# Window attention, forward and backward: another order of work in the opening and in the tail, and later loads

## The chip, the cores and the metric

The kernel runs on one core of one Trainium2 chip. The metric is the device time of one execution in microseconds (us); of several executions the median is given. A profile is taken of a single execution; its "span" reaches from the first to the last instruction of the program, and the execution's own time is a little longer than the span.

The engines: TensorE (PE in the profile; PEld are its weight loads), VectorE (DVE), ScalarE (ACT), GpSimd (POOL) and SyncE (SP). POOL, SP and ACT also issue DMAs, each in its own program order; an instruction that waits holds up everything behind it on its engine.

## The reference

An 8x8 window attention over an image of 256x256 pixels with C = 384 channels, in bf16, with its gradients. x is cut into 1024 windows of 64 tokens.

```python
qkv = xw @ wqkv                       # xw: (1024, 64, 384)
q, k, v = split(qkv)
p = softmax(q @ k.T * C**-0.5)        # per window, 64 x 64
o = (p @ v) @ wo
```

The kernel returns o and, for a given gradient of o, the gradients of x (out_1), of wqkv (out_2, 384x1152) and of wo (out_3, 384x384).

## The kernel before, in words

The weights are folded first: A2 = Wq Wk^T (scaled), A1 its counterpart with q and k exchanged, so the transpose of A2, A3 = wo Wv^T in the form that the gradient needs, and Bm = Wv wo, so the transpose of A3. With these, a window's scores are x A2 x^T, and no q, k or v is ever formed. To fold them, wqkv (w_sb) and wo (wo_sb) are loaded by one DMA each (L68 on SP, L70 on ACT), transposed on TensorE in groups of three 128x128 blocks (L80 to L89; 9 groups for wqkv, 3 for wo, the results in wqkvT_sb and woT_sb), and multiplied (fold, L91 to L104: 9 products for each of the four).

The tokens are worked through in 128 "quads" (NQ) of QT = 4 tiles of 128 tokens (two windows each). A quad needs x_tok and do_tok (4 DMAs of 96 KB each, load_x L123, load_do L128); xdT, both transposed by DMA (front_transpose L135, issued by SP, two DMA transposes); ygT = the products with A2 (first half, from x) and A3 (second half, from do) (front_project L161, 18 products of 512 columns), and yg, its transpose by DMA (L176, three on SP); the scores (front_scores L179); the softmax and its gradient on VectorE with the exponential on ScalarE (front_softmax, front_exp, front_ds); and zb, the products with A1 and Bm (front_zb L225). The back part of a quad forms W and U (back_uw L273), out and dx (back_out L281, which stores them by 6 DMAs on POOL for each of the two) from these. dx needs yg.

The weight gradients are sums over all tokens: G (from U) and F (from W), each in three blocks of 128 rows. weight_grad (L294) is a chain of TensorE products that accumulate in PSUM, four for each quad covered; at the end of a chain the sum is added to G_acc or F_acc in fp32 by VectorE. One of the six blocks (NCH = 6, chains 0 to 2 for G, 3 to 5 for F) is served in each pass, b % 6, over all quads since it was last served: in passes 6 and later 24 products, before that 4 b.

The order of the work is written out by hand (manual_schedule, L331 to L377): each engine executes its instructions in program order. Pass b of the loop (L345) does the back part of quad b and, in between, the front part of quad b + 1, and it asks for the data of quad b + 4: do on POOL at the top of the pass (L349), behind the stores of the pass before; x on SP (L356), behind the DMA transposes of front_transpose(b + 2) and of yg(b + 1). Quads 0 to 3 are loaded ahead of the loop, by POOL (L332 to L340). Pools: 11 buffers for x, 5 for do, 2 for xdT, yg, zb and ygT, 3 each for the staged stores; of PSUM, 3 places (psT, tag "t") that nearly every product and transpose of TensorE goes through.

After the loop the six chains are finished, in the order of how much they have covered (L375); with pass 127 done, 8, 4, 24, 20, 16 and 12 products are left for chains 0 to 5. VectorE casts G_acc and F_acc to bf16 (Gb, Fb, L380, L382), TensorE transposes both (L389), and twelve groups of three products (last, L393) with ScalarE evictions give the gradients of wqkv and wo, which SP stores with four DMAs (L403, L406).

Of the kernel before, what the change touches and what calls it, by code (L numbers as in the profile page):

```python
# [25 lines left out]
def kernel(  # L26
# [32 lines left out]
    psS = ctx.enter_context(tc.tile_pool(name="psS", bufs=1, space=bass.MemoryType.PSUM))  # L59
    psW = ctx.enter_context(tc.tile_pool(name="psW", bufs=1, space=bass.MemoryType.PSUM))  # L60

    mm = nc.tensor.matmul
    tr = nc.tensor.transpose

    ident = const.tile([P, P], BF16)
    make_identity(nc, ident[:])
    w_sb = const.tile([P, CK, J], BF16)
    nc.sync.dma_start(out=w_sb[:], in_=wqkv.rearrange("(m p) j -> p m j", p=P))  # L68
    wo_sb = const.tile([P, CK, C], BF16)
    nc.scalar.dma_start(out=wo_sb[:], in_=wo.rearrange("(m p) n -> p m n", p=P))  # L70
    woT_sb = const.tile([P, CK, C], BF16)
    A1_sb = const.tile([P, CK, C], BF16)
    A2_sb = const.tile([P, CK, C], BF16)
# [2 lines left out]
    big_sb = const.tile([P, JK * C], BF16)  # L76
    wqkvT_sb = big_sb[:].rearrange("p (j c) -> p j c", j=JK)
    dwqkv_sb = big_sb[:].rearrange("p (m j) -> p m j", m=CK)

    for jm in range(JK):  # L80
        ps_t = psT.tile([P, C], BF16, tag="t")
        for m in range(CK):
            tr(ps_t[:, m * P:(m + 1) * P], w_sb[:, m, jm * P:(jm + 1) * P], ident[:])  # L83
        nc.vector.tensor_copy(out=wqkvT_sb[:, jm, :], in_=ps_t[:])
    for mco in range(CK):
        ps_t = psT.tile([P, C], BF16, tag="t")
        for mc in range(CK):
            tr(ps_t[:, mc * P:(mc + 1) * P], wo_sb[:, mc, mco * P:(mco + 1) * P], ident[:])
        nc.vector.tensor_copy(out=woT_sb[:, mco, :], in_=ps_t[:])  # L89

    def fold(dst, lhs, rhs, mul):  # L91
        for i in range(CK):
            ps_c = psT.tile([P, C], F32, tag="t")
            for mc in range(CK):
                mm(ps_c[:], lhsT=lhs(mc, i), rhs=rhs(mc), start=(mc == 0), stop=(mc == CK - 1))  # L95
            nc.scalar.activation(out=dst[:, i, :], in_=ps_c[:], func=ACT.Copy, scale=mul)

    def cut(i):
        return slice(i * P, (i + 1) * P)

    fold(A2_sb, lambda mc, i: wqkvT_sb[:, mc, cut(i)], lambda mc: wqkvT_sb[:, CK + mc, :], scale)
    fold(A3_sb, lambda mc, i: wo_sb[:, mc, cut(i)], lambda mc: wqkvT_sb[:, 2 * CK + mc, :], 1.0)
    fold(A1_sb, lambda mc, i: wqkvT_sb[:, CK + mc, cut(i)], lambda mc: wqkvT_sb[:, mc, :], scale)
    fold(Bm_sb, lambda mc, i: wqkvT_sb[:, 2 * CK + mc, cut(i)], lambda mc: wo_sb[:, mc, :], 1.0)  # L104

    G_acc = const.tile([P, CK, C], F32)
    F_acc = const.tile([P, CK, C], F32)
# [10 lines left out]
        return ap[0, r0:r0 + WIN, c0:c0 + WIN, :]  # L118

    st = [dict() for _ in range(NQ)]  # L120
    vec, act = nc.vector.tensor_copy, nc.scalar.copy

    def load_x(q, eng):  # L123
        st[q]["x"] = x_tok = tokp.tile([P, QT, C], BF16, name="x_tok")
        for t in range(QT):
            eng.dma_start(out=x_tok[:, t, :], in_=dram(x, q, t))
# [8 lines left out]
    def front_transpose(q):  # L135
        s = st[q]
        s["xdT"] = xdT = quad.tile([P, 2, QT, CK, P], BF16, name="xdT")
        for a, src, n in ((0, s["x"], QT), (1, s["do"], QT - PE_T)):
            if n:
                nc.sync.dma_start_transpose(xdT[:, a, 0:n].rearrange("p t m k -> p (t m) k"),  # L140
                                            src[:, 0:n].rearrange("p t c -> p (t c)"))
# [149 lines left out]

    covered = [0] * NCH

    def weight_grad(c, upto, pool, tag):  # L294
        which, acc = (("U", G_acc), ("W", F_acc))[c // CK]
        ma = c % CK
        first = covered[c] == 0
        todo = [(q, t) for q in range(covered[c], upto) for t in range(QT)]
        covered[c] = upto
        if not todo:  # L300
            return
        ps = pool.tile([P, C], F32, tag=tag, name="ps_dw")
        for k, (q, t) in enumerate(todo):
            s = st[q]
            xt = s["xs"][:, t // 2, :] if t % 2 else s["x"][:, t, :]
            mm(ps[:], lhsT=xt[:, cut(ma)], rhs=s[which][:, t, :],  # L306
               start=(k == 0), stop=(k == len(todo) - 1))
            if k == len(todo) - 1:
                if first:
                    nc.vector.tensor_copy(out=acc[:, ma, :], in_=ps[:])  # L310
                else:
                    nc.vector.tensor_tensor(out=acc[:, ma, :], in0=ps[:], in1=acc[:, ma, :], op=ALU.add)
            yield

    def fill(chain, n):
# [13 lines left out]
        front_zb(q, 3)  # L329

    with tc.manual_schedule(engines={ENG.PE, ENG.Activation, ENG.DVE, ENG.Pool, ENG.SP}):  # L331
        load_x(0, nc.gpsimd)  # L332
        load_do(0)
        load_x(1, nc.gpsimd)
        load_do(1)
        front_transpose(0)
        front_transpose(1)
        for q in (2, 3):
            load_x(q, nc.gpsimd)
            load_do(q)  # L340
        front_project(0)
        front_scores(0)
        front_softmax(0)
        zb_phase(0, 1)
        for b in range(NQ):  # L345
            f = b + 1
            ahead = f < NQ
            if b + 4 < NQ:
                load_do(b + 4)  # L349
            if b + 2 < NQ:  # L350
                front_transpose(b + 2)
            back_transpose(b)
            if ahead:
                front_project(f)
            if b + 4 < NQ:
                load_x(b + 4, nc.sync)  # L356
            chain = weight_grad(b % NCH, b, psW, "w")
            half = 2 * QT * min(b, SPAN) // 4
            back_uw(b, "W", 0, act)
            back_uw(b, "W", 1, vec)  # L360
            swap_halves(b)
            fill(chain, half)
            back_uw(b, "U", 0, act)
            back_uw(b, "U", 1, vec)
            back_out(b, "out", 0, act, out_0)
            for _ in chain:
                pass
            back_out(b, "out", 1, act, out_0)
            back_out(b, "dx", 0, vec, out_1)
            back_out(b, "dx", 1, act, out_1)  # L370
            if ahead:
                front_scores(f)
                front_softmax(f)
                zb_phase(f, f + 1 if f + 1 < NQ else None)
        for c in sorted(range(NCH), key=lambda c: covered[c]):  # L375
            for _ in weight_grad(c, NQ, psT, "t"):
                pass  # L377

    Gb = quad.tile([P, CK, C], BF16, tag="yg", name="Gb")
    nc.vector.tensor_copy(out=Gb[:], in_=G_acc[:])  # L380
    Fb = quad.tile([P, CK, C], BF16, tag="yg", name="Fb")
    nc.vector.tensor_copy(out=Fb[:], in_=F_acc[:])  # L382
    GTb = quad.tile([P, CK, C], BF16, tag="zb", name="GTb")
    FTb = quad.tile([P, CK, C], BF16, tag="zb", name="FTb")
    for src, dst in ((Gb, GTb), (Fb, FTb)):
        for mb in range(CK):
            ps_t = psT.tile([P, C], BF16, tag="t")
            for ma in range(CK):
                tr(ps_t[:, cut(ma)], src[:, ma, cut(mb)], ident[:])  # L389
            nc.vector.tensor_copy(out=dst[:, mb, :], in_=ps_t[:])  # L390
    dwo_sb = quad.tile([P, CK, C], BF16, tag="xdT", name="dwo_sb")

    def last(dst, lhs, rhs, mul):  # L393
        ps_e = psT.tile([P, C], F32, tag="t")
        for mb in range(CK):
            mm(ps_e[:], lhsT=lhs(mb), rhs=rhs(mb), start=(mb == 0), stop=(mb == CK - 1))  # L396
        nc.scalar.activation(out=dst, in_=ps_e[:], func=ACT.Copy, scale=mul)

    for ma in range(CK):
        last(dwqkv_sb[:, ma, 0:C], lambda mb: GTb[:, mb, cut(ma)], lambda mb: w_sb[:, mb, C:2 * C], scale)  # L400
        last(dwqkv_sb[:, ma, C:2 * C], lambda mb: Gb[:, mb, cut(ma)], lambda mb: w_sb[:, mb, 0:C], scale)
        last(dwqkv_sb[:, ma, 2 * C:3 * C], lambda mb: FTb[:, mb, cut(ma)], lambda mb: woT_sb[:, mb, :], 1.0)
        nc.sync.dma_start(out=out_2[cut(ma), :], in_=dwqkv_sb[:, ma, :])  # L403
    for mc in range(CK):
        last(dwo_sb[:, mc, :], lambda mb: w_sb[:, mb, 2 * C + mc * P:2 * C + (mc + 1) * P], lambda mb: Fb[:, mb, :], 1.0)
    nc.sync.dma_start(out=out_3.rearrange("(m p) n -> p m n", p=P), in_=dwo_sb[:])  # L406


# [1 line left out]
_INS = ['x', 'wqkv', 'wo', 'grad_out']  # L410
# [26 lines left out]
```

## Time and profile before

| | us |
|---|---|
| time, median of 3 runs (lowest, highest) | 1992.58 (1989.24, 1993.04) |
| the profiled execution's own time | 1991.48 |
| its span | 1989.7 |
| TensorE busy | 1968.0 (99%) |
| VectorE, ScalarE, GpSimd busy | 1454.9, 1213.7, 1129.6 |
| TensorE's first product starts | 6.56 |
| scores of quad 0, 1, 2, 3, 4, 5, 6 start | 20.7, 35.1, 48.4, 61.9, 79.8, 95.2, 109.8 |
| from there on, from scores to scores | 15.20 |
| the last weight gradient product starts | 1976.27 |

How to read it: "busy" of TensorE is modelled from pipelined products, so 99% does not mean that it works at its peak; what can be read from it is where it is not busy. In a line of a timeline there stand the start, the time taken, the engine, the line of the code, the operation, what is written from what, and in brackets how long the engine had been idle and what ended that. Lines with SPq, ACTq and POOL DMA are issues: their time is that of the issuing, and the data land some us later (medians by the page: x by SP 4.2, do 5.1, yg 5.4, xdT 6.3 and 7.1). The granted clock is the share of TensorE's full clock.

### The profile page before, as it was taken

How to read it: one execution, taken by the hardware profiler on the slowest of the kernel's cores; microseconds unless marked ns; L12 is line 12 of the kernel's file. 1: busy time of each engine (PE TensorE's matmuls, PEld its weight loads, DVE VectorE, ACT ScalarE, POOL GpSimd, SP SyncE). 2: the span in 40 equal slices, each digit the busy share in tenths (PEclk: the TensorE clock that was granted, in tenths of full speed). 3: DMA queues.
4: the chain of work that ended last, by engine and by line, in shares of the span. 5: the costliest groups of instructions: out<-in, count | busy, mean ns of one | idle time of the engine just before them, and what ended most of it. 6: DMA issues, size and time to landing. Idle time of an engine off the chain costs nothing.

```text
span 1989.7 us, 52709 instructions
## 1 busy us (share of the span) xinstructions
PE 1968.0 (99%) x20862; PEld 1061.7 (53%) x20862; DVE 1454.9 (73%) x2713; ACT 1213.7 (61%) x1689; POOL 1129.6 (57%) x2070
## 2 busy tenths in 40 slices
PE   7999999999999999999999999999999999999998
PEld 4455555555555555555555555555555555555554
DVE  5777777777777777777777777777777777777774
ACT  5666566566666666665666666666656666666663
POOL 6555555555555655655665555555556555555552
PEclk9999999999999999999999999999999999999999
DMA  9999999999999999999999999999999999999982
GB/s 217 208 216 214 207 213 211 212 213 200 205 208 208 215 213 206 207 214 204 213 206 208 208 208 219 207 197 222 206 206 211 210 202 204 222 206 211 215 175 73
DMA packets 979287, 408.89 MB, mean 206 GB/s; under 512 B 864352, under 2 KB 953440, under 8 KB 979040
## 3 DMA queue, kind: packets, MB, share of 16 engines
q1 hardware_dynamic: 879568, 252.26, 77.8%
q0 software_dynamic: 99072, 152.96, 31.6%
q8 instruction: 164, 2.69, 0.6%
q14 instruction: 83, 0.68, 0.1%
q10 hardware_dynamic: 400, 0.29, 0.0%
HBM read 101.84 MB, written 101.84 MB: 102 GB/s over the span
## 4 chain that ended last, share of the span: by engine, by line
PE 98%; DMA 1%; DVE 1%; ACT 0%; issue 0%
PE ps_dw L306 26%; PE ps_zb L232 26%; PE ps_yg L171 25%; PE ps_dx L257 6%; PE ps_S L187 6%; PE ps_out L257 3%; PE ps_W L257 3%; PE ps_U L257 3%; DMA yg<-ygT 1%; PE ps_c L95 0%; DMA w_sb<-in_wqkv_dram 0%; PE ps_e L396 0%; DVE W_sb L279 0%; PE ps_t L83 0%; DVE ygT L173 0%
## 5 line engine op out<-in xcount | busy, mean ns | idle before, releaser
L286 POOL DMA_DIRECT2D out_dram<-out_sb x256 | 139.2, 544 | 695.4 <-ACT out_sb L285 689.2
L234 ACT CAST zb<-ps_zb 128x768 bf16<-128x768 f32 x512 | 407.6, 796 | 191.7 <-PE ps_zb L232 172.8
L171 PE MATMUL ps_yg<-xdT,A_sb 128*128 128x512 bf16 x2304 | 518.2, 379 | 0.0
L232 PEld LDWEIGHTS <-xdT 128*128 128x128 bf16 x3072 | 290.3, 98 | 188.1 <-issue 1.0
L171 PEld LDWEIGHTS <-A_sb 128*128 128x128 bf16 x2304 | 225.4, 98 | 258.2
L173 ACT CAST ygT<-ps_yg 128x512 bf16<-128x512 f32 (+1 forms) x384 | 280.2, 730 | 92.1 <-PE ps_yg L171 91.0
L232 PE MATMUL ps_zb<-A_sb,xdT 128*128 128x384 bf16 x1536 | 335.1, 327 | 0.0
L232 PE MATMUL ps_zb<-Bm_sb,xdT 128*128 128x384 bf16 x1536 | 333.8, 326 | 0.0
L285 ACT CAST out_sb<-ps_out 128x768 bf16<-128x768 f32 x256 | 205.0, 801 | 151.6 <-issue 143.3
L131 POOL DMA_DIRECT2D do_tok<-in_grad_out_dram x512 | 274.0, 553 | 28.5 <-issue 14.1
L306 PE MATMUL ps_dw<-U_sb,x_tok 128*128 128x384 bf16 x768 | 251.0, 328 | 0.0
L306 PE MATMUL ps_dw<-W_sb,x_tok 128*128 128x384 bf16 x768 | 251.0, 328 | 0.0
L306 PE MATMUL ps_dw<-U_sb,x_sw 128*128 128x384 bf16 x768 | 249.7, 326 | 0.0
L306 PE MATMUL ps_dw<-W_sb,x_sw 128*128 128x384 bf16 x768 | 249.7, 326 | 0.0
L306 PEld LDWEIGHTS <-x_tok 128*128 128x128 bf16 x1536 | 149.6, 97 | 160.1 <-issue 77.1
L279 ACT CAST U_sb<-ps_U 128x768 bf16<-128x768 f32 x128 | 102.1, 798 | 213.8 <-PE ps_U L257 213.8
L247 DVE STREAM_TRANSPOSE pdsT<-pds 32x256 bf16<-32x256 bf16 x512 | 223.2, 436 | 12.0
L306 PEld LDWEIGHTS <-x_sw 128*128 128x128 bf16 x1536 | 150.3, 98 | 82.8
L209 DVE TENSOR_REDUCE rs<-e 128x4 f32<-128x256 f32 x128 | 53.8, 420 | 172.2 <-ACT e L203 172.2
L173 DVE CAST ygT<-ps_yg 128x1024 bf16<-128x1024 f32 x128 | 156.8, 1225 | 29.9 <-PE ps_yg L171 29.3
L288 POOL DMA_DIRECT2D out_dram<-dx_sb x256 | 144.0, 562 | 37.6 <-DMA out_dram<-out_sb 29.7
L287 POOL DMA_DIRECT2D out_dram<-dx_sb x256 | 144.0, 562 | 25.8 <-DMA out_dram<-out_sb 17.5
(71 smaller groups left out, 2596.5 us busy)
## 6 DMA issues: line engine op xcount, KB each, us to landing
do_tok<-in_grad_out_dram POOLq DMA_DIRECT2D x512, 96.0 KB, 5.1
x_tok<-in_x_dram SPq DMA_DIRECT2D x496, 96.0 KB, 4.2
out_dram<-out_sb POOLq DMA_DIRECT2D x256, 96.0 KB, 4.3
out_dram<-out_sb POOLq DMA_DIRECT2D x512, 48.0 KB, 4.3
out_dram<-dx_sb POOLq DMA_DIRECT2D x256, 96.0 KB, 3.7
out_dram<-dx_sb POOLq DMA_DIRECT2D x512, 48.0 KB, 3.8
yg<-ygT SPq DMA_TRANSPOSE x384, 5.4
xdT<-x_tok SPq DMA_TRANSPOSE x128, 6.3
```

Source lines behind the costliest of these rows:

```text
L131: nc.gpsimd.dma_start(out=do_tok[:, t, :], in_=dram(grad_out, q, t))
L171: mm(ps[:, i], lhsT=A_sb[:, m, cut(j)], rhs=s["xdT"][:, a, :, m, :], start=(m == 0), stop=(m == CK - 1))
L173: copy(out=ygT[:, js[0]:js[0] + len(js), :], in_=ps[:, 0:len(js)])
L232: mm(ps[:, i, 0:C], lhsT=s["xdT"][:, 0, t, m, :], rhs=w[:, m, :], start=(m == 0), stop=(m == CK - 1))
L234: nc.scalar.copy(out=s["zb"][:, t], in_=ps[:, :, 0:C])
L247: nc.vector.transpose(out=dst[h + 32 * c:h + 32 * c + 32, :, r, :], in_=src[h + 32 * r:h + 32 * r + 32, :, c, :])
L257: mm(ps[o, b, 0:C], lhsT=lt[i, t, :], rhs=rt(i, t), start=(k == 0), stop=(k == n - 1))
L285: copy(out=o[:], in_=ps[:, :, 0:C])
L286: nc.gpsimd.dma_start(out=dram(dst, q, 2 * p), in_=o[:, 0, :])
L287: nc.gpsimd.dma_start(out=dram_half(dst, q, 2 * p + 1, 1), in_=o[LO, 1, :])
L288: nc.gpsimd.dma_start(out=dram_half(dst, q, 2 * p + 1, 0), in_=o[HI, 1, :])
L306: mm(ps[:], lhsT=xt[:, cut(ma)], rhs=s[which][:, t, :], start=(k == 0), stop=(k == len(todo) - 1))
```

## The change

In the opening:
- w is loaded by three DMAs (its q, k and v columns), still by SP; x(0) is loaded by ACT, and wo after it; the identity is made after these are issued; do(0), x(1), do(1) stay on POOL.
- VectorE fills a tile with zeros, and TensorE does ten products of 384 columns with it into an unused PSUM place.
- wqkv's blocks are transposed third by third (turn_w), copied out by VectorE and ScalarE in turn. A2 is folded after the first two thirds, A3 after the last. A1 and Bm are not folded any more: they are transposed from A2 and A3 on TensorE (turn, three groups each), after the scores of quad 0 and ahead of its zb; so are the three groups of woT. ScalarE copies all nine out.
- POOL copies one column of A3 into the zero tile ahead of the loads of quad 2, so that these wait for A3. Quad 3 isn't loaded ahead of the loop.

In the loop: passes 0 to 5 ask for one quad, b + 3, with x and do both on POOL at the top; pass 6 asks for two, 9 and 10, and from pass 7 on it is b + 4 as before, x on SP.

In the tail: the chains are finished in the order 0 to 5; the last addition of each writes bf16 straight to Gb or Fb, and the two casts go. G is transposed after chain 3, the products of G follow, two after chain 4 and four after chain 5; then F's transposes, the three products for wo's gradient and the three with FTb. Evictions alternate between ScalarE and VectorE, and the stores are five DMAs of SP (three of them of the q and k columns of a row block, one of out_3, one of a v block), and one each of POOL and ACT.

```diff
-    make_identity(nc, ident[:])
-    nc.sync.dma_start(out=w_sb[:], in_=wqkv.rearrange("(m p) j -> p m j", p=P))
-    nc.scalar.dma_start(out=wo_sb[:], in_=wo.rearrange("(m p) n -> p m n", p=P))
-    for jm in range(JK):
...
-        nc.vector.tensor_copy(out=woT_sb[:, mco, :], in_=ps_t[:])
+    def turn(dst, src, copies):
+        for i in range(CK):
+            ps_t = psT.tile([P, C], BF16, tag="t", name="ps_t")
+            for m in range(CK):
+                tr(ps_t[:, cut(m)], src(m, i), ident[:])
+            copies[i % len(copies)](out=dst(i), in_=ps_t[:])
...
-    fold(A2_sb, lambda mc, i: wqkvT_sb[:, mc, cut(i)], lambda mc: wqkvT_sb[:, CK + mc, :], scale)
-    fold(A3_sb, lambda mc, i: wo_sb[:, mc, cut(i)], lambda mc: wqkvT_sb[:, 2 * CK + mc, :], 1.0)
-    fold(A1_sb, lambda mc, i: wqkvT_sb[:, CK + mc, cut(i)], lambda mc: wqkvT_sb[:, mc, :], scale)
-    fold(Bm_sb, lambda mc, i: wqkvT_sb[:, 2 * CK + mc, cut(i)], lambda mc: wo_sb[:, mc, :], 1.0)
+    def turn_w(k):
+        turn(lambda i: wqkvT_sb[:, k * CK + i, :],
+             lambda m, i: w_sb[:, m, k * C + i * P:k * C + (i + 1) * P], (vec, act))
...
-        load_x(0, nc.gpsimd)
+        for k in range(3):
+            nc.sync.dma_start(out=w_sb[:, :, part(k)], in_=wqkv.rearrange("(m p) j -> p m j", p=P)[:, :, part(k)])
+        load_x(0, nc.scalar)
+        nc.scalar.dma_start(out=wo_sb[:], in_=wo.rearrange("(m p) n -> p m n", p=P))
+        make_identity(nc, ident[:])
         load_do(0)
         load_x(1, nc.gpsimd)
         load_do(1)
+        nc.vector.memset(idle_sb[:], 0.0)
+        ps_i = psT.tile([P, C], F32, tag="t", name="ps_i")
+        for _ in range(10):
+            mm(ps_i[:], lhsT=idle_sb[:, 0:P], rhs=idle_sb[:], start=True, stop=True)
         front_transpose(0)
         front_transpose(1)
-        for q in (2, 3):
-            load_x(q, nc.gpsimd)
-            load_do(q)
+        turn_w(0)
+        turn_w(1)
+        fold(A2_sb, lambda mc, i: wqkvT_sb[:, mc, cut(i)], lambda mc: wqkvT_sb[:, CK + mc, :], scale)
+        turn_w(2)
+        fold(A3_sb, lambda mc, i: wo_sb[:, mc, cut(i)], lambda mc: wqkvT_sb[:, 2 * CK + mc, :], 1.0)
+        nc.gpsimd.tensor_copy(out=idle_sb[:, 0:1], in_=A3_sb[:, CK - 1, 0:1])
+        load_x(2, nc.gpsimd)
+        load_do(2)
         front_project(0)
         front_scores(0)
         front_softmax(0)
+        turn(lambda i: A1_sb[:, i, :], lambda m, i: A2_sb[:, m, cut(i)], (act,))
+        turn(lambda i: Bm_sb[:, i, :], lambda m, i: A3_sb[:, m, cut(i)], (act,))
+        turn(lambda i: woT_sb[:, i, :], lambda m, i: wo_sb[:, m, cut(i)], (act,))
         zb_phase(0, 1)
+        loaded = 3
         for b in range(NQ):
...
-            if b + 4 < NQ:
-                load_do(b + 4)
+            early = b < SPAN
+            todo = range(loaded, min(b + (4 if early else 5), NQ))
+            loaded += len(todo)
+            for q in todo:
+                if early:
+                    load_x(q, nc.gpsimd)
+                load_do(q)
...
-            if b + 4 < NQ:
-                load_x(b + 4, nc.sync)
+            for q in todo:
+                if not early:
+                    load_x(q, nc.sync)
...
-        for c in sorted(range(NCH), key=lambda c: covered[c]):
-            for _ in weight_grad(c, NQ, psT, "t"):
+        def flush(c):
+            for _ in weight_grad(c, NQ, psT, "t", Gb if c < CK else Fb):
                 pass
...
-    nc.vector.tensor_copy(out=Gb[:], in_=G_acc[:])
-    nc.vector.tensor_copy(out=Fb[:], in_=F_acc[:])
...
+        for c in range(CK + 1):
+            flush(c)
+        turn(lambda i: GTb[:, i, :], lambda m, i: Gb[:, m, cut(i)], (act,))
+        flush(CK + 1)
+        last_qk(0)
+        flush(CK + 2)
+        last_qk(1)
+        last_qk(2)
+        turn(lambda i: FTb[:, i, :], lambda m, i: Fb[:, m, cut(i)], (act, vec))
+        for mc in range(CK):
+            last(dwo_sb[:, mc, :], lambda mb: w_sb[:, mb, 2 * C + mc * P:2 * C + (mc + 1) * P], lambda mb: Fb[:, mb, :],
+                 1.0, (act, vec, act)[mc])
+        nc.sync.dma_start(out=out_3.rearrange("(m p) n -> p m n", p=P), in_=dwo_sb[:])
+        for ma in range(CK):
+            last(dwqkv_sb[:, ma, part(2)], lambda mb: FTb[:, mb, cut(ma)], lambda mb: woT_sb[:, mb, :],
+                 1.0, (vec, act, vec)[ma])
+            (nc.gpsimd, nc.sync, nc.scalar)[ma].dma_start(out=out_2[cut(ma), part(2)], in_=dwqkv_sb[:, ma, part(2)])
```

weight_grad gets an argument out, to which the last addition is written in place of acc; last takes the engine of its eviction; last_qk(ma) does the q and the k product of row block ma, evicts one by ScalarE and one by VectorE, and stores both by one DMA of SP.

More of the change, by code (lines that the diff above doesn't have):

```diff
@@ L60 @@
     psW = ctx.enter_context(tc.tile_pool(name="psW", bufs=1, space=bass.MemoryType.PSUM))
+    vec, act = nc.vector.tensor_copy, nc.scalar.copy
     mm = nc.tensor.matmul
@@ L78, with cut, part @@
     dwqkv_sb = big_sb[:].rearrange("p (m j) -> p m j", m=CK)
-    for jm in range(JK):
[L81 to L88, printed above, removed]
-        nc.vector.tensor_copy(out=woT_sb[:, mco, :], in_=ps_t[:])
+    idle_sb = const.tile([P, C], BF16)
+    def cut(i):
+        return slice(i * P, (i + 1) * P)
+    def part(i):
+        return slice(i * C, (i + 1) * C)
+    def turn(dst, src, copies):
[4 more added lines that the diff above has]
+            copies[i % len(copies)](out=dst(i), in_=ps_t[:])
     def fold(dst, lhs, rhs, mul):
         for i in range(CK):
-            ps_c = psT.tile([P, C], F32, tag="t")
+            ps_c = psT.tile([P, C], F32, tag="t", name="ps_c")
             for mc in range(CK):
@@ L96, in fold @@
             nc.scalar.activation(out=dst[:, i, :], in_=ps_c[:], func=ACT.Copy, scale=mul)
-    def cut(i):
-        return slice(i * P, (i + 1) * P)
-    fold(A2_sb, lambda mc, i: wqkvT_sb[:, mc, cut(i)], lambda mc: wqkvT_sb[:, CK + mc, :], scale)
-    fold(A3_sb, lambda mc, i: wo_sb[:, mc, cut(i)], lambda mc: wqkvT_sb[:, 2 * CK + mc, :], 1.0)
-    fold(A1_sb, lambda mc, i: wqkvT_sb[:, CK + mc, cut(i)], lambda mc: wqkvT_sb[:, mc, :], scale)
-    fold(Bm_sb, lambda mc, i: wqkvT_sb[:, 2 * CK + mc, cut(i)], lambda mc: wo_sb[:, mc, :], 1.0)
+    def turn_w(k):
+        turn(lambda i: wqkvT_sb[:, k * CK + i, :],
+             lambda m, i: w_sb[:, m, k * C + i * P:k * C + (i + 1) * P], (vec, act))
     G_acc = const.tile([P, CK, C], F32)
@@ L120 @@
     st = [dict() for _ in range(NQ)]
-    vec, act = nc.vector.tensor_copy, nc.scalar.copy
     def load_x(q, eng):
@@ L292, with weight_grad @@
     covered = [0] * NCH
-    def weight_grad(c, upto, pool, tag):
+    def weight_grad(c, upto, pool, tag, out=None):
         which, acc = (("U", G_acc), ("W", F_acc))[c // CK]
@@ L308, in weight_grad @@
             if k == len(todo) - 1:
+                to = acc if out is None else out
                 if first:
-                    nc.vector.tensor_copy(out=acc[:, ma, :], in_=ps[:])
+                    nc.vector.tensor_copy(out=to[:, ma, :], in_=ps[:])
                 else:
-                    nc.vector.tensor_tensor(out=acc[:, ma, :], in0=ps[:], in1=acc[:, ma, :], op=ALU.add)
+                    nc.vector.tensor_tensor(out=to[:, ma, :], in0=ps[:], in1=acc[:, ma, :], op=ALU.add)
             yield
@@ L374 @@
                 zb_phase(f, f + 1 if f + 1 < NQ else None)
-        for c in sorted(range(NCH), key=lambda c: covered[c]):
-            for _ in weight_grad(c, NQ, psT, "t"):
-                pass
-    Gb = quad.tile([P, CK, C], BF16, tag="yg", name="Gb")
-    nc.vector.tensor_copy(out=Gb[:], in_=G_acc[:])
-    Fb = quad.tile([P, CK, C], BF16, tag="yg", name="Fb")
-    nc.vector.tensor_copy(out=Fb[:], in_=F_acc[:])
-    GTb = quad.tile([P, CK, C], BF16, tag="zb", name="GTb")
-    FTb = quad.tile([P, CK, C], BF16, tag="zb", name="FTb")
@@ L385 @@
[L385 to L405, printed above, removed]
@@ L406 @@
-    nc.sync.dma_start(out=out_3.rearrange("(m p) n -> p m n", p=P), in_=dwo_sb[:])
+        Gb = quad.tile([P, CK, C], BF16, tag="yg", name="Gb")
+        Fb = quad.tile([P, CK, C], BF16, tag="yg", name="Fb")
+        GTb = quad.tile([P, CK, C], BF16, tag="zb", name="GTb")
+        FTb = quad.tile([P, CK, C], BF16, tag="zb", name="FTb")
+        dwo_sb = quad.tile([P, CK, C], BF16, tag="xdT", name="dwo_sb")
+        def flush(c):
+            for _ in weight_grad(c, NQ, psT, "t", Gb if c < CK else Fb):
+                pass
@@ new lines, in last, with last_qk @@
+        def last(dst, lhs, rhs, mul, copy):
+            ps_e = psT.tile([P, C], F32, tag="t", name="ps_e")
+            for mb in range(CK):
+                mm(ps_e[:], lhsT=lhs(mb), rhs=rhs(mb), start=(mb == 0), stop=(mb == CK - 1))
+            if copy is act:
+                nc.scalar.activation(out=dst, in_=ps_e[:], func=ACT.Copy, scale=mul)
+            else:
+                nc.vector.tensor_scalar_mul(out=dst, in0=ps_e[:], scalar1=mul)
+        def last_qk(ma):
+            last(dwqkv_sb[:, ma, part(0)], lambda mb: GTb[:, mb, cut(ma)], lambda mb: w_sb[:, mb, part(1)], scale, act)
+            last(dwqkv_sb[:, ma, part(1)], lambda mb: Gb[:, mb, cut(ma)], lambda mb: w_sb[:, mb, part(0)], scale, vec)
+            nc.sync.dma_start(out=out_2[cut(ma), 0:2 * C], in_=dwqkv_sb[:, ma, 0:2 * C])
```

## The prediction

> **What bounds the kernel now.** I read the page's chain first, then the timelines of the opening and the end, then the waits, then SP's own timeline.
>
> ```profile
> PE 98%; DMA 1%; DVE 1%; ACT 0%; issue 0%
> PE ps_dw L306 26%; PE ps_zb L232 26%; PE ps_yg L171 25%; PE ps_dx L257 6%; PE ps_S L187 6%; PE ps_out L257 3%; PE ps_W L257 3%; PE ps_U L257 3%; DMA yg<-ygT 1%; PE ps_c L95 0%; DMA w_sb<-in_wqkv_dram 0%; PE ps_e L396 0%; DVE W_sb L279 0%; PE ps_t L83 0%; DVE ygT L173 0%
> ```
>
> TensorE is the chain. From the sixth pass on, the scores (L187) start every 15.20 us, without exception, to the end. The change leaves these passes alone, so it can only win in the first 110 us and the last 27. There the chain names two things that are not TensorE: `yg<-ygT`, 1% though one stall made it, and the first weights.
>
> The opening, TensorE's timeline (start, us, what):
>
> ```profile
> 6.56 3.06 PE L83 MATMUL ps_t<-ident,w_sb 128*128 128x128 bf16 x27 [6.56 <-DMA w_sb<-in_wqkv_dram]
> 9.43 1.15 PE L88 MATMUL ps_t<-ident,wo_sb 128*128 128x128 bf16 x9
> 10.39 2.13 PE L95 MATMUL ps_c<-big_sb 128*128 128x384 bf16 x9
> ...
> 16.75 4.05 PE L171 MATMUL ps_yg<-xdT,A_sb 128*128 128x512 bf16 x18
> ```
>
> It waits 6.56 us for the weights, then works without a hole to the first projection; scores start at 20.72, the first zb at 22.58, the second projection at 26.49.
>
> The early stall, TensorE's and then SP's timeline:
>
> ```profile
> 78.83 0.36 PE L257 MATMUL ps_dx<-yg,pds 64*64 64x384 bf16 x4 [3.47 <-DMA yg<-ygT]
> ```
>
> ```profile
> 58.15 2.36 SPq L140 DMA_TRANSPOSE xdT<-x_tok  x1
> 60.70 3.02 SPq L140 DMA_TRANSPOSE xdT<-do_tok  x1
> 63.81 6.64 SPq L176 DMA_TRANSPOSE yg<-ygT  x3
> 70.50 3.10 SPq L126 DMA_DIRECT2D x_tok<-in_x_dram  x4
> ```
>
> The dx products of pass 3 wait 3.47 us for yg(3), which SP began to issue only at 63.81, though its ygT had been evicted by 58.6: SP was still at an x load and two transposes. SP issues back to back from 20 to 200 us. After the stall the granted clock is half from 79.69 to 83.10 (3.41 us): 1.7 us more. The stall costs 5.2.
>
> The end, a timeline:
>
> ```profile
> 1976.27 0.33 PE L306 MATMUL ps_dw<-U_sb,x_sw 128*128 128x384 bf16 x1
> ...
> 1978.04 0.68 PE L389 MATMUL ps_t<-ident,Gb 128*128 128x128 bf16 x9 [1.45 <-DVE Gb L380]
> ...
> 1984.89 1.47 ACT L397 ACTIVATE dwo_sb<-ps_e 128x384 bf16<-128x384 f32 x3
> 1986.38 0.38 SPq L406 DMA_DIRECT2D out_dram<-dwo_sb  x1
> ```
>
> TensorE waits for two casts on VectorE, then twelve products are paced by ScalarE's 0.49 us evictions.
>
> **Opening.** Before scores(0), 18 fold products (A1, Bm; 18 x 0.163 = 2.9 us) and nine transposes of wo go. w in thirds brings the first columns sooner; x(0), now issued by ScalarE ahead of wo, is no longer behind all of w, so its transpose on SP starts near 6 instead of 7.97. The weight path (nine groups of transposes, copied alternately by VectorE, 0.32 us, and ScalarE, taken as 0.49 from the 128x384 evictions, then two folds of 1.5) is done by about 12 and lies beside the next wait: the projection's second half needs the transposed do(0). By 8.94 before had landed w, wo, x(0) and do(0); the same bytes go first after, so do(0) lands near 8.9. Its transpose took 3.2 us to issue (9.77 to 12.96), and the one of x(0) landed 3.8 us after its issue ended (9.60; the trace marks its completion at 13.44, and so for every landing below). I take 14 for the landing, a little under 8.9 + 3.2 + 3.8 because fewer loads compete; ends 13 and, as in before, 16.8. Half a projection is 2.0 us, so scores(0) start at 16 (15 to 18.8), against 20.72: 4.7 us sooner.
>
> Behind the scores now stand 27 transposes in nine groups (A1, Bm, woT), each with a ScalarE copy. With three PSUM buffers the first zb gets its place after the seventh copy: 7 x 0.49 + 0.25 = 3.7 us that before did not have there. No row shows ScalarE copying bf16 from PSUM; bounds are VectorE's 0.32 and ScalarE's 0.62 for 512 columns, so 2.5 to 4.6; 0.49 is the same engine and width. Net for the opening: **-1.0 us** (-3.2, from 15 and 2.5, to +2.7, from 18.8 and 4.6). exp(0) moves with the first zb copy, so the softmax chain shifts along and adds nothing.
>
> The ten idle products (0.32 each, as the folds before 11.42 are apart: 3.2 us, from about 1.2) lie before any weight lands: nothing, and at most 0.5 if the first third lands at 4. They bring the full clock sooner than 11.42, worth up to 2.4 us (36 transposes at 0.053 saved, and three products), but under the wait for do(0): nothing in the sum; if that cover is gone because do(0) is early, it is what keeps the weight path out of the way.
>
> [...]
>
> POOL's new wait (a one-column copy that needs A3's last eviction, near 12) queues behind it x(2), do(2), x(3), do(3); xdT(2) needs the former, for a projection that started at 39.87. Nothing.
>
> **Loads.** At any pass below 6 one quad (x and do, 0.79 MB) less has been asked for: at 206 GB/s 3.8 us of traffic out of yg(3)'s way. x(4) to x(8) leave SP, 2.5 to 3.7 us per pass that it no longer spends ahead of the transposes. POOL gets them: 20 issues per pass instead of 16, 11.0 us of some 13.4; it fits, but out writes queue behind. So yg(3), landed at 78.8, lands at 75.0 or sooner; needed at 75.01 - 1.0. I take the stall and its half clock as gone: **-5.2 us** (0 to -5.2).
>
> Pass 6 then issues two quads, x(9) and x(10) on SP, and by pass 7 the traffic asked for equals before's. There before had little room: the landing of yg(8) (149.65) against its dx (154.31) is 4.7 us, that of xdT(9) (142.48) against the second half of its projection (146.97) is 4.5. TensorE would arrive 1.0 + 5.2 = 6.2 us sooner, so 6.2 - 4.5 = 1.7 is given back: **+1.7** (0 to +5.2, a stall as at 75 us with its half clock).
>
> **Tail.** The 84 remaining weight products (8, 4, 24, 20, 16, 12 by chain) keep their 0.163 us; sums go straight to bf16, so two casts go, and G's transposes and products run between F's chains. From 1962.78: four chains to 1971.9; the third transpose group waits for the F sum's 0.56 us eviction: 1972.95; chain and two products to 1976.5, chain to 1978.5, four products to 1980.4; F's transposes wait for two evictions: 1981.45; six products and the last 0.55 us eviction to 1985.2. The last DMA is issued there instead of 1986.38; its 2.3 us to land (1986.38 to 1988.67) and what follows stay: **-1.2 us** (-0.3 to -2).
>
> **The sum.** The profiled execution took 1991.48 us (span 1989.7 and 1.8 around it), 1.1 below the median of the three shown, 1992.58. 1991.5 - 1.0 - 5.2 + 1.7 - 1.2 = 1985.8; I say **1986.0**.
>
> **Rivals.**
> - *The transfers stay as late as they were.* DMA share is 1.17 to 1.24 from 10 to 50 us, and between 72 and 74 us only 42 GB/s moved though packets were outstanding: what delays yg(3) may be the engines, not SP's order. Then the opening's gain and the deferral go into the stall, and only the tail is left: 1991.5 - 1.2 = 1990.3. For it: POOL and SP were both held by landings at 68 to 78. An opening that loses would only shorten the stall. Against: 3.8 us of traffic really are gone, and the share is 1.12 to 1.16 later too, where nothing waits.
> [...]
> - *Nothing is given back.* The early throughput dip does not recur, pass 6's double load is hidden, the opening has its 2.0: 1991.5 - 2.0 - 5.2 - 1.2 = 1983.1, and with 0.8 more from the tail 1982.3.
> - *Slower: the double load.* x(9), x(10), do(9), do(10) in one pass put 3.8 us into a queue with 4.5 of room while TensorE is 6.2 ahead; if passes 7 to 9 each then stall as pass 3 did (3.47 and 1.7), 3 x 5.2 replaces the 1.7: 1984.1 + 15.6 = 1999.7. It decides from the second such stall on (10.4 against a gain of 7.4). Against: backlog that stalls once has the stall to catch up.
>
> **Chances.** Forecast 0.50, transfers as late 0.24, nothing given back 0.18, double load 0.08. Against the median, 0.2% (4 us, about what a measurement can tell) puts faster below 1988.6: forecast and third case, and a little of the first rival's edge, 0.70; within 0.22; slower 0.08. The range takes in 1990.3 and 1982.3 with 0.7 or 0.8 beyond each: 1981.5 to 1991.0.
>
> **What would show it.** Scores(0) near 16 and zb(0) near 21.5: the opening. No wait for `yg<-ygT` above 1 us before 80, no half clock after the opening: the loads. A wait for yg or xdT between 110 and 150: what is given back. The last DMA issue 1.2 us sooner after the last chain starts: the tail. Wrong if xdT(0) of do lands after 17, or SP is still back to back at 60 us.

## The result, and the profile after

The changed kernel takes **1997.08 us** in the median (1993.79 to 2001.15, 13 executions), the kernel before 1991.87 (1988.47 to 1994.32, 13 executions on the same chip): a ratio of **1.0033, interval 1.0025 to 1.0042**. That is slower by 5 to 8 us; I had forecast 1986.0, and 1981.5 to 1991.0 as the range.

The profiled execution took 1997.38 us, its span 1995.6, 5.9 longer than before. Taken apart by the starts of the scores (pass 3 here is from scores(3) to scores(4), as in the prediction):

| from scores to scores, us | before | after | difference |
|---|---|---|---|
| start to scores(1) | 35.07 | 36.23 | +1.2 |
| passes 1 and 2 | 13.4 each | 13.4 each | 0 |
| pass 3 | 17.93 | 13.93 | -4.0 |
| pass 4 | 15.43 | 13.97 | -1.5 |
| pass 5 | 14.56 | 17.82 | +3.3 |
| pass 6 | 15.20 | 16.58 | +1.4 |
| pass 8 | 15.20 | 19.19 | +4.0 |
| scores(127) to the end | 40.33 | 41.87 | +1.5 |

Every other pass takes what it took, 15.20. The stall of pass 3 did go, as predicted; 8.6 us came back in passes 5, 6 and 8 where I had put 1.7. And the tail, whose order I had counted as a gain, is longer.

The chain of waits of the changed kernel, its share by engine:

```profile
PE 95%; DMA 2%; DVE 1%; ACT 1%; issue 0%; POOL 0%; ACTq 0%; SPq 0%; POOLq 0%
```

TensorE has 95% where it had 98%; a second percent of DMA, ACT and a little of POOL, which was not in the chain at all, have come in.

*The opening.* TensorE's timeline and then SP's (start, time taken, what, and in brackets the idle time before it and what ended that):

```profile
9.88 0.68 PE L90 MATMUL ps_t<-ident,w_sb 128*128 128x128 bf16 x9 [1.45 <-DMA w_sb<-in_wqkv_dram]
11.88 1.64 PE L97 MATMUL ps_c<-big_sb,wo_sb 128*128 128x384 bf16 x9 [1.32 <-DMA wo_sb<-in_wo_dram]
14.70 4.06 PE L168 MATMUL ps_yg<-xdT,A_sb 128*128 128x512 bf16 x18 [1.19 <-DMA xdT<-x_tok]
18.68 0.60 PE L184 MATMUL ps_S<-xdT,ygT 128*64 128x64 bf16 x26
```

```profile
10.16 1.60 SPq L137 DMA_TRANSPOSE xdT<-x_tok  x1
11.94 2.48 SPq L137 DMA_TRANSPOSE xdT<-do_tok  x1
```

The first transpose of x(0) is issued at 10.16, not near 6 and even later than before (7.97): x(0) shares the transfers with the three thirds of w and with do(0), which land until 9.83 and 9.50, and its own fourth tile lands at 10.08. It is x(0)'s transpose that the first projection waits for (1.19 us, to 14.70); behind that it runs without a wait for do(0)'s. Scores(0) start at 18.68. The 27 transposes and their copies then put 3.2 us ahead of zb(0) (scores to zb 5.07 against 1.86), so zb(0) starts at 23.75, 1.2 later than before.

*Pass 5.* ScalarE's, TensorE's and POOL's timelines:

```profile
95.94 0.80 ACT L282 CAST dx_sb<-ps_dx 128x768 bf16<-128x768 f32 x1 [4.89 <-DMA out_dram<-dx_sb]
```

```profile
96.79 0.65 PE L229 MATMUL ps_zb<-A_sb,xdT 128*128 128x384 bf16 x3 [2.86 <-ACT dx_sb L282]
```

```profile
86.16 0.56 POOL L284 DMA_DIRECT2D out_dram<-out_sb  x1 [1.84 <-DMA do_tok<-in_grad_out_dram]
86.73 0.56 POOL L285 DMA_DIRECT2D out_dram<-out_sb  x1
89.38 0.54 POOL L283 DMA_DIRECT2D out_dram<-dx_sb  x1 [2.09 <-DMA do_tok<-in_grad_out_dram]
```

Read from the bottom: POOL's stores wait for the landing of a load of do that POOL itself had issued ahead of them; so the staging buffer comes free late, ScalarE stands 4.89 us at the dx eviction with zb's eviction behind it, and TensorE 2.86 us for its PSUM place. Pass 6 shows the same with 1.22 us.

Why should a store wait for a load? By the trace POOL's 2081 DMAs signal their landing on eight semaphores in turn (260 or 261 on each), and of 1814 for which the landing of the one eight issues ahead is known none starts before it, while 269 start before the one seven ahead has landed. In the kernel before it is the same (eight semaphores, 258 on each; none of 1542), but there four loads stand ahead of the twelve stores of a pass; here eight do, and so each of the next eight stores has a load eight issues ahead of it. The store at 89.38 waited for a load of do that was issued at 78.35 and landed at 88.83. That load was slow, too: for two of these microseconds the transfers moved 43 GB/s (a row of the stretches table; its last two columns are DMA share and GB/s).

```profile
81.00:83.00 2.00, 2.00 (x12) 1.00 (x11) 1.86 (x5) 1.82 (x3) 0.57 (x1) 1.00 1.31 43
```

*Pass 8* is another wait, for the second half of a projection; a stretch of 71 GB/s, from 146 to 148 us, stands ahead of it:

```profile
149.60 1.67 PE L168 MATMUL ps_yg<-xdT,A_sb 128*128 128x512 bf16 x4 [2.14 <-DMA xdT<-do_tok]
```

*The tail.* First the timeline of the last stores, then POOL's instructions on the program's last line, after and before (durations in ns, minimum, median and maximum; then the first and the last start in us):

```profile
1988.68 0.60 POOL L436 DMA_DIRECT2D out_dram<-big_sb  x1 [16.35 <-DVE big_sb L413]
1988.80 0.56 DVE L413 TENSOR_SCALAR big_sb<-ps_e 128x384 bf16<-128x384 f32 x1 [0.42 <-PE ps_e L409]
1988.83 0.33 SPq L436 DMA_DIRECT2D out_dram<-big_sb  x1
1989.39 0.36 ACTq L436 DMA_DIRECT2D out_dram<-big_sb  x1
```

```profile
L461 POOLq DRAIN  x3: 40/102/6180, 1988.7 to 1995.4; - x3
```

```profile
L432 POOLq DRAIN  x3: 40/102/5390, 1966.7 to 1989.4; - x3
```

The last DMA is issued 35.6 us after scores(127), against 37.0 before: 1.4 us sooner, near the 1.2 that I had predicted. But POOL ends its program with a drain behind its last DMA, of 5.39 us before and 6.18 after. Before, that DMA was a store of the loop, and the drain (1966.7 to 1972.1) lay under the last chains. Now POOL has one of the last stores, the drain runs from 1988.7 to 1994.8, and all else waits for it: the last drains of the other four engines start at 1995.1 to 1995.2, though the stores had landed by 1991.2.

### The profile page after: what moved, and what is told of

It reads as the page before. It is cut to its first block, busy times and chain, and to the rows that moved or that the text cites. A ratio compares the mean times of both kernels' runs of the same rounds, so it can differ in the third digit from the quotient of the medians.

```text
span 1995.6 us, 52746 instructions
## 1 busy us (share of the span) xinstructions
PE 1970.3 (99%) x20872; PEld 1061.0 (53%) x20872; DVE 1454.0 (73%) x2707; ACT 1214.4 (61%) x1694; POOL 1139.1 (57%) x2088
## 3 DMA queue, kind: packets, MB, share of 16 engines
q1 hardware_dynamic: 877632, 250.10, 77.4%
q0 software_dynamic: 99888, 154.63, 31.7%
## 4 chain that ended last, share of the span: by engine, by line
PE 95%; DMA 2%; DVE 1%; ACT 1%; issue 0%; POOL 0%; ACTq 0%; SPq 0%; POOLq 0%
PE ps_dw L303 26%; PE ps_zb L229 25%; PE ps_yg L168 25%; PE ps_dx L254 6%; PE ps_S L184 5%; PE ps_out L254 3%; PE ps_W L254 3%; PE ps_U L254 3%; DMA do_tok<-in_grad_out_dram 1%; DMA out_dram<-dx_sb 1%; DMA xdT<-do_tok 0%; DMA x_tok<-in_x_dram 0%; PE ps_e L409 0%; DVE W_sb L276 0%; DMA xdT<-x_tok 0%
## 5 line engine op out<-in xcount | busy, mean ns | idle before, releaser
L170 DVE CAST ygT<-ps_yg 128x1024 bf16<-128x1024 f32 x128 | 156.8, 1225 | 31.7 <-PE ps_yg L168 31.3
```

The costliest lines, as they stand in the source:

```text
L170: copy(out=ygT[:, js[0]:js[0] + len(js), :], in_=ps[:, 0:len(js)])
```

## The experiments

All ratios are to the kernel before on the same chip in the same series; 0.001 is 2.0 us. The intervals are about 2 us wide to either side, so a difference of two kernels below some 3 us is not settled by them.

**The store of POOL.** e1: the changed kernel, `(nc.gpsimd, nc.sync, nc.scalar)[ma]` becomes `(nc.sync, nc.sync, nc.scalar)[ma]`.

> The changed kernel, its one store of the tail that POOL issues given to SP. Theory: in the changed kernel POOL's own end-of-program drain begins after that store (1988.66) and lasts 6.2 us, to 1994.84, while the last store had landed by 1991.3; without it the end follows the landing, 3 us sooner: 1994 against 1997.1. Rival: the end is late because the stores are spread over three queues and the last one is ACT's; then the time stays at 1997.

Measured: 1.0007 (0.9997 to 1.0017), 5.2 us less than the change. The drain is back under the chains (POOL's timeline: 1971.0 to 1977.7, 6.7 us). Passes 5, 6 and 9 still lose 0.7, 5.0 and 1.2 us, the 5.0 from a wait of 3.12 us for dx_sb and a half clock behind it (mean 0.91 from 100 to 120 us).

e4, the reverse: the kernel before, and only `out_3` stored by `nc.gpsimd`.

> The kernel before, its last store (of out_3) issued by POOL instead of SP, nothing else. Theory: POOL's drain, which lay at 1966.73 to 1972.12 under the last chains, now begins behind this store, at 1987, and lasts 5.4 to 6.2 us: 3.5 to 4 us more than before, 1995.5. Rival: a POOL store lands like an SP store (2.0 and 2.3 us), and nothing changes: 1992.

Measured: 1.0015 (1.0002 to 1.0027), +3.0 us. Its drain, 5.05 us, runs from 1984.0 to 1989.1, and scores(127) to the end takes 43.06, 2.7 more than before. The drain is shown from both sides, at 3 to 5 us.

**The tail's order alone.** e3: the kernel before with the new tail, the last stores by SP and ACT.

> The kernel before with the new tail only, POOL's store of it given to SP. Theory: the order of the tail is worth what it shows up to the last issue (22.24 us after the first remaining chain starts instead of 23.60), 1.4 us less than before: 1990.5. Rival: the order itself is what lengthens the end by 1.5: 1993.4.

Measured: 0.9989 (0.998 to 0.9997), -2.2 us: better than either theory. In the three kernels below that have this tail without a half clock in it (e12, f3, f4), scores(127) to the end is 38.28, 38.31 and 38.55 us against 40.33: -1.8 to -2.0.

**Who issues x.** e2: the changed kernel, x by SP in passes 0 to 5 too, POOL's last store kept.

```diff
-                if early:
-                    load_x(q, nc.gpsimd)
                 load_do(q)
...
-                if not early:
-                    load_x(q, nc.sync)
+                load_x(q, nc.sync)
```

> The changed kernel, x of passes 0 to 5 issued by SP behind the projection's transposes as in the kernel before; still one quad later, still two in pass 6. Theory: with 20 issues per pass POOL falls behind, stores go out late, and in passes 5 and 6 an eviction waits 2.9 and 1.2 us for a store buffer; that goes, 4 to 5 us less than the changed kernel: 1992.5 to 1993. Rival: the engines' total traffic sets passes 5 to 8, whoever issues x: 1996 to 1998, with the waits at another tile.

Measured: 1.0059 (1.0045 to 1.0072). The theory that x on POOL is all of it fell. Instead of the store buffers, TensorE waits six times for xdT between 90 and 170 us, 10.9 us in all (waits of TensorE in that window):

```profile
PE ps_yg L168 <- DMA xdT<-do_tok: 6.8, 3, 4.1
PE ps_yg L168 <- DMA xdT<-x_tok: 4.1, 3, 2.1
```

x of quad b+3 then is asked for in the middle of pass b and transposed at the top of pass b+1. So two things had been changed together: who issues x, and how far ahead. The next kernels part them.

**Parts alone.** e5: opening alone. e6: loads alone. e7: all but the loads (SP's last store).

> The new opening alone (weights in thirds, A1 and Bm by transposes behind the scores, idle products, x(0) issued by ScalarE); loads two quads ahead as before, tail as before. In the changed kernel the second projection began 1.15 us later than before. If the opening is that cost and no more, the time is 0 to 1.2 us above the kernel before (the pass-3 stall, which waits for a transfer and not for TensorE, takes some of the 1.15 back), and the stall at dx(3) is there at about 3 us. Rival: the opening's own gain carries through (scores(0) 2 us sooner) and the time is 1 to 2 us below before.

> The new loads alone: quad 3 not loaded ahead, in passes 0 to 5 quad b+3 with x by POOL, two quads in pass 6; opening and tail as before. Theory (the deferral and POOL's 20 issues move the stall instead of taking it away): the wait at dx(3) is gone, but passes 5 to 9 show at least 4 us of TensorE waits for dx_sb's store or for xdT; the time is 1 to 3 us above before. Rival (what I predicted): the stall's 5.2 us go and 1.7 come back, so 3.5 us below before.

> Everything of the change but the loads, which go two quads ahead with x by SP as before; the last store of out_2 by SP. Sum of the parts so far: tail -2.2 (measured alone), opening 0 to +1.2: 1 to 2.2 us below before, at least 2 us under the changed kernel with SP's store (1.0007 of before). Rival, if the loads were not the loss: the same as that kernel, 1 us above before or more.

Measured: e5 1.0008 (1.0 to 1.0017), +1.5 us, but not in the way I expected: no wait at dx(3); the first projection waits 2.35 and 1.48 us for xdT(0), whose transposes now run beside the loads of quads 2 and 3, and the clock is half from 16.3 to 23.1 (mean 0.91 in the first 40 us). e6 1.0011 (1.0 to 1.0023), +2.2 us, as the theory said, though with only 2.4 us lost in passes 7 and 8 of the profiled execution and 2.7 in pass 2. e7 0.9987 (0.9978 to 0.9996), -2.6 us: without the new loads the change is a gain.

**Lead or POOL.** e8: e1 with quads 2 and 3 both loaded behind A3 and then always b+4, x still by POOL in passes 0 to 5. e12: the same, x by SP.

```diff
-        load_x(2, nc.gpsimd)
-        load_do(2)
+        for q in (2, 3):
+            load_x(q, nc.gpsimd)
+            load_do(q)
...
-            todo = range(loaded, min(b + (4 if early else 5), NQ))
+            todo = range(loaded, min(b + 5, NQ))
```

> The changed kernel with SP's last store and without the holding back: quads 2 and 3 go behind A3 and then always quad b+4, but x still by POOL in passes 0 to 5. It parts two causes of the waits in passes 5 to 9. If holding back (less lead) is the cause, they go and the time is that of the kernel with the loads of before, 1 to 2 us below before. If POOL's 20 issues per pass are the cause, the waits for dx_sb's store stay, 3 to 6 us in passes 4 to 7, and the time is 1 to 3 us above before.

> Quads 2 and 3 loaded behind A3, then always quad b+4 with x by SP behind yg: it differs from the kernel with no deferral and x by POOL (1.0008 of before) only in who issues x in passes 0 to 5. If POOL's issues cost, this one is 2 to 4 us faster than that, so 0.5 to 2.5 us below before. If the transfers set the time, it is within 1.5 us of it, with a stall of 2 to 4 us in one of the passes 1 to 4.

Measured: e8 1.0008 (0.9996 to 1.002), e12 0.9989 (0.998 to 0.9997): with the same bytes, x by SP is 3.8 us faster (give or take 3, by the two intervals), and e12's trace has no wait of TensorE above 0.8 us from 20 us to the end. What POOL waits for between 30 and 130 us (wait: us in all, times, longest), in the changed kernel and in e12:

```profile
POOL out_dram L283 <- ACT out_sb L282: 10.2, 2, 8.8
POOL out_dram L284 <- DMA do_tok<-in_grad_out_dram: 4.8, 4, 1.8
...
POOL out_dram L283 <- DMA do_tok<-in_grad_out_dram: 2.1, 1, 2.1
```

```profile
POOL out_dram L283 <- ACT out_sb L282: 30.3, 8, 8.4
```

In e12 POOL waits 30 us for ScalarE to give it something to store: once in every pass it is ahead. In the changed kernel that has shrunk to two waits, and the stores wait for POOL's own loads to land. e8 shows the latter too, but not what I expected to follow from it: no wait for dx_sb's store ends at its TensorE. Its waits, POOL's and then TensorE's:

```profile
POOL out_dram L284 <- DMA do_tok<-in_grad_out_dram: 6.6, 6, 2.3
```

```profile
PE ps_dx L254 <- DMA yg<-ygT: 3.7, 2, 2.6
```

TensorE lost its time there in pass 2, to yg(2), with 6.8 us at half clock beside it; SP began to issue yg(2)'s transposes at 47.84, beside eight loads that POOL issued from 44.57 to 49.4, and from 50 to 54 us the transfers moved 33 and 69 GB/s. e1 shows the other way again (3.12 us for dx_sb, behind 57 GB/s from 96 to 98 us). So with x by POOL beside do the profiles show two ways in which time is lost, late stores and late transposes; how the 3.8 us divide between them is not settled. e12 has such slow stretches too (62 GB/s from 70 to 72 us) and loses nothing to them.

f4 completes the table of two by two: b+3, x by SP, SP's last store (e2 with e1's edit).

> The changed kernel with x by SP in passes 0 to 5, quad b+3, and SP's last store: with the other three it fills a table of two by two (who issues x; b+3 or b+4), tail and opening the same. If one quad less of lead costs only where SP issues x late in the pass, it is 6 us or more above the kernel that holds nothing back with x by SP (0.9989), so 1.002 or more; xdT waits in passes 4 to 9. If holding back costs nothing, as it did with x by POOL (1.0007 against 1.0008), it is within 1.5 us of 0.9989, and POOL's drain was the whole loss of the first such kernel (1.0059).

Measured: 1.0067 (1.0053 to 1.0081), with 13.8 us of waits for xdT.

| tail and opening new, SP's last store | x by SP | x by POOL |
|---|---|---|
| always b+4 | 0.9989 (e12) | 1.0008 (e8) |
| b+3 in passes 0 to 5 | 1.0067 (f4) | 1.0007 (e1) |

Holding one quad back costs some 15 us where SP brings x in the middle of a pass, and nothing more where POOL brings it at the top beside do, which costs 3.8 us by itself.

**Count or place.** f3: as e8, but in passes 0 to 5 SP issues do in the place where it otherwise issues x (load_do gets an argument for the engine), so that POOL has 16 issues per pass and not 20.

```diff
                 if early:
                     load_x(q, nc.gpsimd)
-                load_do(q)
+                else:
+                    load_do(q)
...
-                if not early:
+                if early:
+                    load_do(q, nc.sync)
+                else:
                     load_x(q, nc.sync)
```

> As the kernel with no deferral and x by POOL in passes 0 to 5 (1.0008 of before), but in these passes SP issues do in the place where it issues x in the kernel with x by SP (0.9989): POOL has 16 issues per pass again, the traffic is the same. If it is POOL's count that costs 3.8 us, this is within 1.5 us of 0.9989. If it is that x is brought by POOL at the top of a pass, beside the transposes, it stays at 1.0005 or more.

Measured: **0.9983 (0.9975 to 0.9992)**, 1987.19 us in the median against 1991.9. x at the top of the pass by POOL is harmless; four loads more there, eight in all ahead of POOL's twelve stores, are what costs (5.0 us against e8, give or take 3). Whether that is by their number in POOL's program or by coming at once, ahead of SP's transposes, the swap doesn't tell: it takes both away. f3 has no wait of TensorE above 0.8 us from 20 us to the end, though the transfers fall to 30 GB/s from 52 to 54. It has the lowest ratio found, 3.4 us below the kernel before, and some 10 below the changed one; e3, e7 and e12 lie within its interval.

e11 (on e1) had tried to give POOL room from the other side: the out stores of passes 0 to 5 by ScalarE.

> The changed kernel with SP's last store, and the six out stores of each of the passes 0 to 5 issued by ScalarE, so that POOL issues 14 per pass and not 20; the traffic is the same. If POOL's issues are the cause, the waits in passes 5 to 9 go and the time falls to 1 to 3 us below before. If the transfers are, waits of 4 us or more in all stay between 60 and 170 us, and the time stays within 1.5 us of the same kernel with these stores on POOL (1.0007 of before).

Measured: 1.0063 (1.0051 to 1.0076). It tells nothing of POOL, since it made ScalarE the bound: its timeline shows the issues between its evictions,

```profile
55.14 0.60 ACTq L284 DMA_DIRECT2D out_dram<-out_sb  x1
55.78 0.61 ACTq L285 DMA_DIRECT2D out_dram<-out_sb  x1
56.43 0.61 ACTq L286 DMA_DIRECT2D out_dram<-out_sb  x1
57.22 0.80 ACT L282 CAST dx_sb<-ps_dx 128x768 bf16<-128x768 f32 x1 [2.11 <-DMA out_dram<-out_sb]
```

and six such issues of 0.6 us per pass make passes 1 to 6 some 1.8 to 3.4 us longer.

**Is it the transfers?** e9 (on e1) and e10 (on the kernel before): stores of passes 0 to 5 cut to one eighth, as many DMAs as ever; the rest of out and dx of these quads is left out.

```diff
+        if q < 6:
+            nc.gpsimd.dma_start(out=dram(dst, q, 2 * p)[0:2], in_=o[0:16, 0, :])
+            nc.gpsimd.dma_start(out=dram_half(dst, q, 2 * p + 1, 1)[0:1], in_=o[LO, 1, :][0:8])
+            nc.gpsimd.dma_start(out=dram_half(dst, q, 2 * p + 1, 0)[0:1], in_=o[HI, 1, :][0:8])
+            return
```

> The changed kernel with SP's last store, and the out and dx stores of passes 0 to 5 cut to one eighth of their rows (the same number of DMAs, issued by POOL in the same order; seven eighths of out_0 and out_1 of the first six quads are left out). Theory now: the transfer engines are full in the opening and passes 0 to 5, whose work is 13.4 to 14.5 us long against 15.20 later, and every form of the loads pays for that. Then the waits between 60 and 170 us go: scores(12) at about 197 instead of 203.7, the time 6 to 7 us below the same kernel with all stores (1.0007 of before). Rival: POOL's 20 issues per pass, which stay, are the cause; then the waits for dx_sb's store or xdT stay and scores(12) come after 201.

> The kernel before with the same cut of the stores of passes 0 to 5. Theory (transfers): the 3.5 us wait of pass 3 and the half clock behind it go, scores(12) at about 195.7 instead of 201.0, the time 4 to 5.3 us below before. Rival (what I predicted: SP's own order, an x load and two transposes ahead of yg(3)): SP's order is unchanged, so the stall stays at 2 to 3.5 us and the time is at most 2 us below before.

Measured: e9 0.9986 (0.9977 to 0.9995), 4.2 us below e1, without a wait in passes 1 to 12. e10 0.9997 (0.9988 to 1.0006): no stall in its trace either, but only 0.6 us gained by the ratio, where the theory wanted 4 or more. Less traffic does help e9, with POOL's 20 issues left in place; but that the transfers are a floor under the early passes fell, with e12, which moves all the bytes (224 GB/s from 30 to 130 us; the changed kernel 201) and has no stall.

**Is the stall of pass 3 a fixed thing?** f1 and f2: the kernel before, unchanged, two more profiles.

> The kernel before, unchanged, profiled once more. My prediction took the stall of its pass 3 (3.47 us at 75, yg(3) late because SP was late) for a fixed part of its time. If so, the same wait of 3 us or more stands in pass 3 again. New theory: it was a chance event, two microseconds in which the transfer engines moved 49 GB/s (72 to 74 us) with packets outstanding; such stretches come in all profiles, about 1.3 per 100 us; then pass 3 takes under 15 us here, or a stall stands in another pass.

> The same once more: fixed order, the stall of 3 us or more is in pass 3 again; chance, it is elsewhere or missing in at least one of the two.

Measured: 1998.16 and 1988.77 us. In f1 the dx products of pass 3 wait even longer; in f2 pass 3 takes 13.86 us and has no such wait:

```profile
83.46 0.53 PE L257 MATMUL ps_dx<-yg,pds 64*64 64x384 bf16 x4 [4.45 <-DMA yg<-ygT]
```

e3 and e4, whose opening and loads are those of before, bear on it too: pass 3 takes 18.51 and 13.86 us. So three of five executions have the stall, and the one that I predicted from held one draw of something that varies. What goes with it is a stretch in which the transfers nearly stop while DMA engines have work. The stretches table of the kernel before and of f2, same stretch:

```profile
72.00:74.00 2.00, 1.80 (x20) 0.86 (x18) 1.92 (x4) 1.43 (x2) 0.00 (x0) 1.00 0.97 42
```

```profile
72.00:74.00 2.00, 2.00 (x16) 0.75 (x15) 1.78 (x5) 1.18 (x2) 1.04 (x2) 1.00 1.07 233
```

Counted by the ends of the packets from 20 us on, 25 two-microsecond stretches of the kernel before moved less than 90 GB/s, 22 of them after 200 us, where no pass lost anything; 18 to 33 there in the other kernels. In f1 the one at 76 to 78 us (71 GB/s) precedes its stall. They hurt only in the early passes, which are 13.4 to 14.6 us long for the traffic of a 15.20 us pass; that this is the reason fits, but no run tests it. What makes these stretches was not found.

## Why the prediction was wrong, step by step

The sum was -1.0 - 5.2 + 1.7 - 1.2. Three steps failed, and two more terms were off in size.

- **The tail: "its 2.3 us to land and what follows stay".** They did not. The last DMA is earlier as forecast (1.4), and the order is worth 1.8 to 2.2, the far end of my range. But I looked only at when the last DMA is issued, not at which engine issues it. Giving one store to POOL put its drain at the end: +3.0 (e4) to +5.2 (e1). The row was there to be read: POOL's instructions on the program's last line in the trace of before, 5.39 us, hidden.
- **Loads: "it fits, but out writes queue behind".** 20 issues of 0.55 us do fit into 13.4 us as time, and POOL is busy only 65 of the 100 us from 30 to 130. What does not fit is the waiting: POOL's stores wait for the landing of the loads eight issues ahead of them (none of 1814 of its DMAs started sooner), and in the changed kernel and e1 the stores hold ScalarE's buffers, and so zb. I had named the queue and priced it at nothing; x by POOL beside do costs 3.8 us (e8 against e12), and the swap takes it back (f3). That all of it goes by the stores is not shown: e8's own wait is for yg.
- **Loads: "I take the stall and its half clock as gone: -5.2".** It is gone in the changed kernel, but the kernel before has it in some executions and not in others (4.45 us in f1, none in pass 3 of f2), so a median does not hold all of it; e10 gains 0.6. My range's upper end, 0, covered this; my value took one draw for a rule. SP's order, which I made the cause, is the same in f2, which has no stall; that it decides what a slow stretch of the transfers hits is an inference.
- **"+1.7" for the double load of pass 6.** The place was partly right (the wait for xdT(9) at 149.60, 2.14 us and a half clock, 4.0 in pass 8), the size was not, and passes 5 and 6 lost 4.6 more by the step above. That the double load brings the wait of pass 8 is not shown: the stretch of 71 GB/s stands ahead of it, and e1, with the same double load, waits 0.99 us in pass 9 and not in pass 8. The slower rival, a double load that stalls passes 7 to 9, came near in size but by another mechanism: the waits of passes 5 and 6 (ended at 96.79 and 112.96) lie before that load is asked for.
- **Opening: -1.0.** The transposes behind the scores cost 3.2, where I had 3.7. The failed term is "its transpose on SP starts near 6": 10.16, because ScalarE's DMAs of x(0) share the transfers with w and do(0) from the start (last landings 10.08, 9.83 and 9.50); so the wait that ends last is the one for x(0)'s transpose and not, as I had it, for do(0)'s. Scores(0) gained 2.0, not 4.7. In the profile it is +1.2; by the medians the new opening with the loads held is worth nothing (e12 and e3, both 0.9989), so the step was off by about 1 to 2 us, within its bounds. The full clock came at 6.48 us, where it had come at 11.42; the wait up to 14.70 lies over that, so it shows in no term.

The runs give the ledger by differences of their ratios: tail's order -2.2, POOL's last store +5.2, x by POOL beside do +3.8, one quad less of lead -0.2 in that company, opening 0: together +6.6, what 1.0033 says. The terms were read one behind the other from these same kernels, so that they add up is no check; e4, e7 and f3 are.

The rival of late transfers came nearest to the stall's cause: a slow stretch stands ahead of it in all three executions that have it (42 GB/s before, 71 in f1, 55 in e3). But who issues a load is not all one to the time. SP's and POOL's queues take 77.4% and 31.7% of the same 16 DMA engines in the changed kernel, and still the kernel took 3.8 us more when POOL issued the same bytes (e8 against e12): what stands behind an issue in that engine's program can wait with it, as the changed kernel's store at 89.38 did for 2.09 us.

## What to carry to other kernels

Look at the end of each engine's program, not only at the last DMA: an engine with a slow end-of-program drain, as POOL's of 5.39 and 6.18 us here, should issue its last DMA well before the end. Before loads are moved to an engine that also stores, read how long that engine waits for work in each pass; when that wait is gone, its stores are late, and what is late next are the buffers behind them. A stall in a single profile may be a draw: take a second and a third profile before its whole length goes into a sum.

## What was not expected of the hardware

- POOL's drain at the end of the program took 5.39 us in the kernel before, 6.18 in the changed one, 6.69 in e1 and 5.05 in e4, under the last chains (before, e1) as well as behind the last stores. In these four traces SP's took 7 to 13 ns, ScalarE's and VectorE's at most 0.60 us, TensorE's up to 0.93.
- The granted clock fell to half for 3.41 us (149.84 to 153.25) behind an idle time of only 2.14 us, ended at 149.60; behind 2.86 us, ended at 96.79 of the same execution, it stayed at 1.00. The granted clock of the changed kernel (the column before DMA share), in the stretches before and behind that wait:

```profile
146.00:149.60 3.60, 1.47 (x7) 0.59 (x6) 3.12 (x7) 1.43 (x3) 1.10 (x2) 1.00 1.27 161
149.70:153.10 3.40, 3.40 (x9) 1.03 (x8) 0.00 (x0) 1.01 (x1) 3.23 (x7) 0.52 1.24 301
```

Such spells stand in other traces too: the mean clock is 0.91 from 100 to 120 us in e1 and from 80 to 100 in e3, 0.83 from 60 to 80 in e8, and 0.91 and 0.92 from 40 to 60 in e5 and e7, where TensorE is busy for 19.04 of these 20 us. By my estimate one costs 1.7 us (half of 3.41), and a part of the few microseconds between executions of one kernel is this: of the eleven of f3 the fastest, 1985.43 us, had a mean clock of 1.000, the slowest, 1989.5, 0.997. What brings the spells was not found.
